# One planner, two orders: keeping column-tiled matmuls together in an agent-attention and SoLU-FFN kernel on Trainium2

## The chip, the cores and the metric

The kernel runs on one core of one Trainium2 chip. That core has a matrix engine (TensorE; the profile lists its matmuls as PE and its weight loads as PEld), three engines for elementwise work (VectorE as DVE, ScalarE as ACT, GpSimd as POOL) and a queue engine that issues all DMAs (SyncE as SP). Each engine executes its own instructions in the order in which they stand in the program. TensorE writes its results to PSUM, from where DVE and ACT read them. The metric is the device time of one execution in microseconds (us); less is better.

## The reference

Four batches, each with 12608 tokens of width 128. Stage one is agent attention with 49 agents per batch, stage two a feed-forward layer of width 1024 with a softmax-weighted activation (SoLU) and a layer norm:

```python
scale = 1.0 / np.sqrt(q.shape[-1])
def sm(a, b):
    s = scale * (a @ b.transpose(0, 2, 1))
    s = s - s.max(-1, keepdims=True)
    e = np.exp(s)
    return e / (e.sum(-1, keepdims=True) + 1e-09)
agent_v = sm(agents, k) @ v            # (4, 49, 128): over 12608 keys
x = (sm(q, agents) @ agent_v).reshape(B * S, D)

h = x @ w_in                           # (50432, 1024)
e = np.exp(h - h.max(-1, keepdims=True))
solu = h * e / (e.sum(-1, keepdims=True) + 1e-09)
mu = solu.mean(-1); var = ((solu - mu) ** 2).mean(-1)
out = ((solu - mu) / np.sqrt(var + 1e-06) * g_ln) @ w_out
```

Inputs and output are float32; `w_in` and `w_out` come as float64 words that the kernel converts itself (`pair_f64`).

## The kernel before, in words

The tokens are cut into 396 tiles of 128, 99 per batch. Three groups of steps are interleaved.

**The agents' stage (`phase_a`)** goes over the keys and values of one batch in 13 chunks of 1024 (the last has 320 keys). For chunk `c`: `p1_mm` (L418) multiplies agents and keys, `p1_max` and `p1_nm` (L423 to L430) keep a running maximum, `p1_exp` (L444) takes the exponentials, `p2_t` (L451) transposes them on TensorE, `p2_et` (L457) copies the transposed block out of PSUM on ACT or DVE, `p2_mm` (L467) multiplies with the values and `p2_ev` (L474, L476) adds it to the sum. At the end the sum is multiplied with `w_in` (`f3`, L531), so that the matrix of stage two already holds the agents' values. For batch 0 this stage runs alone, ahead of everything else: the head. For batches 1 to 3 it is woven into the tiles of the batch before.

**The queries' stage (`phase_b`)** goes over units of 8 tiles. `b0` (L647) multiplies 8 tiles of queries with the agents, `b1` to `b4` are the softmax, `b5` (L682) transposes, and DMAs lay the result out as `pT` (L706).

**The feed-forward stage** is done tile by tile: `c_h` (L747) makes h in PSUM, `c_max` (L751) the row maximum on DVE, `c_exp` (L761) on ACT, `c_u` (L766) on DVE, `c_sq` (L772) on ACT, `c_t` (L779) transposes u in eight blocks on TensorE, `c_ev` (L794, L798) copies on ACT, the parts are split into a high and a low half (L803 on DVE, L807 and L811 on POOL), and `c_w` (L827) does 24 matmuls with `w_out` for each pair of tiles.

On TensorE these steps use the array in two ways. `p1_mm`, `p2_mm` and `b0` write 64 of the 128 output rows with each matmul, two matmuls side by side: the array is tiled in columns, and the profile shows them as 128*64. All others (`c_h`, `c_w` and the transposes) use the whole array, shown as 128*128. The program numbers the kinds: 0 for `c_h` and `c_w`, 1 for transposes and a few small matmuls, 2 for the three column-tiled steps.

The order is made by a planner that runs when the program is built (class `Plan`). Each step is an `Op` with an engine, a planned duration (`cost`), a due time (`due`), the steps it waits for, and the PSUM bank that it takes or frees. `run` walks all engines: for each it looks at the steps that could start, keeps those that could start within `EPS[e]` of the earliest, and takes the one that is due first; of the engines, the one whose step starts first. After a TensorE step it adds `SWITCH[kind before][kind now]` to the planned duration. The order found so is the program's order on each engine; the chip then waits on semaphores alone. Planned durations and due times therefore set the order and nothing else; no instruction gets longer or shorter by them. Due times are built from constants such as `BD0` to `BD5` (queries' stage), `DH`, `DMX`, `DEX` and the like (tile steps), `ASTART` and `AEND` (agents' stage).

In the head the planner also puts filler matmuls (L918, into a PSUM tile that nobody reads) where it plans TensorE to stand idle, as many as fill 0.7 of the planned gap. The head further holds the conversion of both weights from float64 words (`pair_f64`, L263: per weight 18 instructions on DVE, 2 on ACT, 4 on POOL). `load_out` issues the load of `w_out` after the loads of chunk `VA`; the conversion of `w_out` must end before `c_exp` of the first two tiles, since it uses their buffers.

PSUM has four banks (`px`) for everything but h: `c_w` holds one over two pairs of tiles, and the column-tiled steps, the transposes and the small matmuls share the rest.

## Time and profile before

| | us |
|---|---|
| median of 3 runs | 1548.81 (1548.41 to 1549.6) |
| the profiled execution, its own time | 1548.65 |
| its span in the profile | 1546.9 |

The profiled execution's time is 1.75 us more than its span. Its stages, from the timeline: the head lasts to 62 us, where the first `c_h` stands; batches 0 to 2, each with the next batch's agents' stage woven in, last to about 1200 us; batch 3 has no agents' stage beside it and lasts to the end. The granted TensorE clock is 1.00 in every stage. A row of the timeline gives the start of the first of several equal instructions, the time from there to the end of the last, and their count. Matmuls are pipelined, each lasts longer than the distance to the next: what a matmul costs the engine is the distance between starts, not the duration in the row.

### The profile page before, as it was taken

The numbers are of one execution on the slowest core, as the hardware profiler recorded it, in microseconds if no ns is written. First come the engines' busy times: TensorE is split into PE (matmuls) and PEld (weight loads), VectorE is DVE, ScalarE is ACT, GpSimd is POOL, SyncE is SP. The second block draws the span as 40 slices with busy tenths as digits, with TensorE's granted clock in tenths as the row PEclk, the third lists the DMA queues.
The fourth block names the chain that finished last, engine by engine and source line by source line (L and its number), as shares of the span: only waits on it lengthen the run. The fifth ranks groups of instructions, "written<-read, shape, count | busy, mean of one in ns | idle before, by whom it ended". The sixth has DMA issues, their size and how long they took to land.

```text
span 1546.9 us, 35512 instructions
## 1 busy us (share of the span) xinstructions
PE 1526.4 (99%) x12628; PEld 1356.1 (88%) x12628; DVE 1372.4 (89%) x2214; ACT 1421.6 (92%) x2738; POOL 1252.9 (81%) x1613
## 2 busy tenths in 40 slices
PE   8899999999999999999999999999999999999998
PEld 4588898998889889898898889898889999999998
DVE  6988998888898889898898889889899999999997
ACT  3599999999899999999999999999999999999997
POOL 1478878787888887888878887887788899898987
PEclk9999999999999999999999999999999999999999
DMA  9533333324233333332333334433222232222221
GB/s 370 186 104 100 107 98 115 117 69 127 81 97 118 103 110 117 112 102 83 106 98 101 111 97 117 116 100 105 78 76 75 68 90 76 71 82 70 68 62 46
DMA packets 114721, 159.65 MB, mean 103 GB/s; under 512 B 16240, under 2 KB 71152, under 8 KB 114544
## 3 DMA queue, kind: packets, MB, share of 16 engines
q1 hardware_dynamic: 114544, 157.39, 34.0%
q8 instruction: 100, 1.64, 0.4%
q14 instruction: 77, 0.63, 0.1%
HBM read 105.36 MB, written 26.02 MB: 85 GB/s over the span
## 4 chain that ended last, share of the span: by engine, by line
PE 95%; DVE 3%; ACT 1%; DMA 1%; issue 0%; SPq 0%; DVEq 0%; ACTq 0%
PE px L827 36%; PE ph L747 24%; PE px L779 23%; PE px L647 3%; PE px L467 3%; PE px L418 3%; PE px L451 1%; PE px L682 1%; PE px L531 0%; DMA pT<-pn 0%; DVE mxp L423 0%; DVE nm L751 0%; DMA kh<-in_kT_dram 0%; DVE ca_in L263 0%; DVE uL L803 0%
## 5 line engine op out<-in xcount | busy, mean ns | idle before, releaser
L811 POOL TENSOR_TENSOR uL<-uT,uH 128x1024 fp32r<-128x1024 f32 (+1 forms) x344 | 661.5, 1923 | 27.6
L751 DVE TENSOR_REDUCE nm<-ph 128x1 f32<-128x1024 f32 x396 | 481.3, 1217 | 50.5 <-PE ph L747 47.7
L766 DVE SCALAR_TENSOR_TENSOR u<-ph,e 128x1024 f32<-128x1024 f32 x396 | 479.0, 1217 | 34.6 <-ACT e L761 24.4
L772 ACT ACTIVATE sq<-u,su 128x1024 bf16<-128x1024 f32 x396 | 460.5, 1163 | 24.8 <-DVE u L766 20.4
L761 ACT ACTIVATE e<-ph,nm 128x1024 f32<-128x1024 f32 x396 | 445.9, 1128 | 31.9 <-DVE nm L751 30.7
L827 PE MATMUL px<-uL,wH 128*128 128x256 f32 x1584 | 466.9, 295 | 0.2 <-POOL uL L811 0.2
L827 PE MATMUL px<-uH,wH 128*128 128x256 f32 x1584 | 450.6, 284 | 1.8 <-DVE uL L803 1.8
L827 PE MATMUL px<-uH,wL 128*128 128x256 f32 x1584 | 448.1, 283 | 0.0
L779 PE MATMUL px<-ident,u 128*128 128x128 f32 x3168 | 425.5, 274 | 2.7 <-DVE uL L803 1.4
L779 PEld LDWEIGHTS px<-ident,u 128*128 128x128 f32 x3168 | 356.7, 141 | 55.2 <-issue 20.7
L807 POOL TENSOR_SCALAR uH<-uT 128x1024 fp32r<-128x1024 f32 (+1 forms) x344 | 298.3, 867 | 98.4 <-ACT uT L798 98.0
L747 PE MATMUL ph<-mh,pT 128*128 128x512 f32 x792 | 329.7, 416 | 1.6 <-DMA pT<-pn 1.3
L827 PEld LDWEIGHTS px<-uH,wH 128*128 128x128 f32 x1584 | 299.0, 189 | 16.9 <-issue 3.5
L747 PE MATMUL ph<-ml,pT 128*128 128x512 f32 x792 | 312.3, 394 | 0.0
L798 ACT COPY uT<-px 128x512 f32<-128x512 f32 x541 | 299.2, 589 | 11.9 <-PE px L779 3.0
L827 PEld LDWEIGHTS px<-uH,wL 128*128 128x128 f32 x1584 | 299.1, 189 | 8.6 <-issue 0.7
L827 PEld LDWEIGHTS px<-uL,wH 128*128 128x128 f32 x1584 | 298.9, 189 | 8.5 <-issue 4.6
L803 DVE TENSOR_TENSOR uL<-px,uH 128x512 fp32r<-128x512 f32 x251 | 168.8, 685 | 47.5 <-ACT uH L794 45.8
L747 PEld LDWEIGHTS ph<-mh,pT 128*128 128x128 f32 x792 | 149.3, 188 | 20.3 <-issue 3.4
L747 PEld LDWEIGHTS ph<-ml,pT 128*128 128x128 f32 x792 | 149.9, 189 | 17.7 <-issue 0.5
L794 ACT CAST uH<-px 128x512 fp32r<-128x512 f32 x251 | 143.7, 592 | 1.2 <-PE px L779 0.9
L846 POOL TENSOR_TENSOR y<-x,nhalf 128x4 f32<-128x4 f32 x99 | 100.1, 1011 | 7.7
(118 smaller groups left out, 1337.6 us busy)
## 6 DMA issues: line engine op xcount, KB each, us to landing
pT<-pn SPq DMA_DIRECT2D x392, 64.0 KB
rB<-dr SPq DMA_DIRECT2D x98, 256.0 KB
qt<-in_qT_dram SPq DMA_DIRECT2D x48, 512.0 KB
out_dram<-ob SPq DMA_DIRECT2D x95, 256.0 KB
kt<-in_kT_dram SPq DMA_DIRECT2D x36, 512.0 KB
vt<-in_v_dram SPq DMA_DIRECT2D x36, 512.0 KB
dr<-yr SPq DMA_DIRECT2D x392, 0.5 KB
kh<-in_kT_dram SPq DMA_DIRECT2D x12, 512.0 KB
```

Of the source, the lines that this page charges most:

```text
L747: nc.tensor.matmul(ph[:, sl], lhs, bmats[b]["mh" if m == 0 else "ml"][:, sl], start=(m == 0), stop=(m == 1))
L751: nc.vector.tensor_reduce(out=nms[x], in_=phs[x], op=ALU.max, axis=AX.X, negate=True)
L761: nc.scalar.activation(out=es[x], in_=phs[x], func=AF.Exp, bias=nms.pop(x), accum_out=st[G]["S"][:, j : j + 1])
L766: nc.vector.scalar_tensor_tensor(out=u, in0=phs[x], scalar=INV, in1=es[x], op0=ALU.mult, op1=ALU.mult, accum_out=su)
L772: nc.scalar.activation(out=sq, in_=u, func=AF.Square, bias=su, scale=-float(DF), accum_out=st[G]["Q"][:, j : j + 1])
L779: nc.tensor.transpose(pt[:, kf * P : (kf + 1) * P], us[x][0][:, k0 * P : (k0 + 1) * P], ident)
L794: nc.scalar.copy(out=uH, in_=pt)
L798: nc.scalar.copy(out=rr[x][:, hf * 4 : hf * 4 + 4, :], in_=pt)
L803: nc.vector.tensor_tensor(out=uL, in0=pt, in1=uH.bitcast(F32), op=ALU.subtract)
L807: nc.gpsimd.tensor_scalar(out=uH, in0=rr[x][:, k0:k1, :], scalar1=1.0, scalar2=0.0, op0=ALU.mult, op1=ALU.add)
L811: nc.gpsimd.tensor_tensor(out=uL, in0=rr[x][:, k0:k1, :], in1=uH.bitcast(F32), op=ALU.subtract)
L827: nc.tensor.matmul(po, wt[:, kf, :], ut[:, kf, :], start=(q == 0), stop=(q == WM - 1))
```

## The change

The planner gets a new rule and new numbers. The rule: when TensorE's last planned step was column-tiled (kind 2), the planner first looks for column-tiled steps that could start within `HOLD` = 0.17 of the earliest step of any kind, and takes one of those if there is one. `SWITCH` now charges for going into column tiling (0.12) and for leaving it (0.18 and 0.14), and nothing for staying. The planned costs of the three column-tiled steps are set anew, and three of the conversion's DVE steps are planned at 0.9 for 0.6. The agents' stage of batches 1 to 3 is no longer spread evenly from `ASTART` to `AEND`: chunk `c` is due `UB * ASP` = 6.8 tiles after the one before, and its `p2_mm` is due later in that step (`MZ` = 2.36 for 1.5, where the next chunk's `p1_mm` stands at 2.55). `w_out` is loaded after chunk 9 for 7, `w_in` ahead of all keys (`WA`), the conversion of `w_in` is due after the agents' stage of batch 0 (`CPR`), not before it. Most of the other due times are new numbers.

```diff
--- before.py
+++ after.py
@@ -30,7 +30,9 @@
            "AA": 0.0, "AG": 0.17, "GP": 0.25, "GD": 0.1, "GG": 0.1, "GA": 0.2}
     EPS = {"P": 0.01, "A": 0, "D": 0.07, "G": 2.6, "S": 0.0}
 
-    SWITCH = ((0.0, 0.0, 0.0), (0.0, 0.0, 0.0), (0.087, 0.033, 0.033))
+    SWITCH = ((0.0, 0.0, 0.12), (0.0, 0.0, 0.12), (0.18, 0.14, 0.0))
+
+    HOLD = 0.17
 
     def __init__(self, banks):
         self.banks = [[0.0, b] for b in banks]
@@ -78,7 +80,10 @@
                     low = s if low is None else min(low, s)
                 if low is None:
                     continue
-                s, o = min((z for z in opts if z[0] <= low + self.EPS[e]), key=lambda z: z[1].due)
+                near = [z for z in opts if z[0] <= low + self.EPS[e]]
+                if e == "P" and self.kind == 2:
+                    near = [z for z in opts if z[0] <= low + self.HOLD and z[1].kind == 2] or near
+                s, o = min(near, key=lambda z: z[1].due)
                 if o.shy > 0.0:
                     s, o = min((z for z in opts if z[0] <= s + o.shy), key=lambda z: z[1].due)
                 if best is None or s < best[0]:
@@ -148,7 +153,7 @@
     CKT = N - NCK * CT * P
     AP2 = 64
     ETE = "AD"
-    CPR = -1.98
+    CPR = 1.32
     UTB = 4
     DIR = {(1, 0), (1, 1), (3, 1), (5, 1), (7, 1)}
     LGC = 8
@@ -156,56 +161,58 @@
     TD = 2
     WC = 4
 
-    BD0 = 13.69
-    BD1 = 8.27
-    BD2 = 9.96
-    BD3 = -18.57
-    BD4 = 0.41
-    BD5 = 5.85
-    DH = -3.05
-    DMX = -3.31
-    DEX = 7.76
-    DU_ = 6.48
-    DSQ = 21.68
+    BD0 = 14.77
+    BD1 = 12.82
+    BD2 = 19.94
+    BD3 = -16.84
+    BD4 = 0.17
+    BD5 = 4.61
+    DH = -3.24
+    DMX = 6.49
+    DEX = 0.49
+    DU_ = -2.17
+    DSQ = 18.46
     DT = -0.42
-    DEV = -6.42
-    DLD = 1.96
-    DSP = 2.68
-    DW = 3.31
-    DR = 2.33
-    DF_ = 5.14
-    OUTD = -5.86
+    DEV = -7.32
+    DLD = 2.24
+    DSP = -1.16
+    DW = 3.3
+    DR = 15.18
+    DF_ = 5.63
+    OUTD = -4.87
     OUTC = -74.58
-    VA = 7
+    VA = 9
     VA1 = 12
-    QA = 8
-    WA = 0.5
-    VLAG = 0.25
+    QA = 5.64
+    WA = -5.59
+    VLAG = 0.61
     PTB = 8
-    SHY = -2.99
-    DHR = -4.59
-    DHL = -5.42
-    DMXR = 10.02
-    DMXL = 15.46
-    DEXR = 5.1
-    DEXL = -1.93
-    DUR = -10.64
+    SHY = -0.0
+    DHR = -4.39
+    DHL = -5.43
+    DMXR = -0.03
+    DMXL = 10.25
+    DEXR = 23.76
+    DEXL = -1.81
+    DUR = -10.37
     DUL = -12.84
     DSQR = -10.36
     DSQL = -12.17
     DTR = -6.53
-    DTL = -23.81
-    DEVR = -0.65
+    DTL = -23.89
+    DEVR = -12.92
     DEVL = 9.51
     DLDR = -16.59
     DLDL = 26.96
     DSPR = -6.09
-    DSPL = 14.43
-    DWR = 0.63
+    DSPL = 14.3
+    DWR = 2.02
     DWL = -0.21
     RBL = 6.0
-    ASTART = -3.67
-    AEND = -2.04
+    ASP = 0.85
+    MZ = 2.36
+    ASTART = -3.92
+    AEND = -6.25
     engs = (mybir.EngineType.PE, mybir.EngineType.Activation, mybir.EngineType.DVE, mybir.EngineType.Pool)
     SCALE = 1.0 / math.sqrt(C)
     INV = 1.0 / DF
@@ -273,10 +280,10 @@
             + op("D", ts, "s", 0.34, in0="e", scalar1=23, scalar2=None, op0=SL)
             + op("D", ts, "a", 0.34, in0="hi", scalar1=12, scalar2=9, op0=SL, op1=SR)
             + op("G", gt, "r", 1.23, in0="r", in1="s", op=ALU.mult)
-            + op("D", tt, "a", 0.6, in0="s", in1="a", op=ALU.bitwise_or)
-            + op("D", stt, "a", 0.6, in0="lo", scalar=29, in1="a", op0=SR, op1=ALU.bitwise_or)
+            + op("D", tt, "a", 0.9, in0="s", in1="a", op=ALU.bitwise_or)
+            + op("D", stt, "a", 0.9, in0="lo", scalar=29, in1="a", op0=SR, op1=ALU.bitwise_or)
             + op("G", gt, "d", 1.23, in0="r", in1="a", op=ALU.add)
-            + op("D", stt, "di", 0.6, in0="hi", scalar=-(2 ** 31), in1="di", op0=ALU.bitwise_and, op1=ALU.bitwise_or)
+            + op("D", stt, "di", 0.9, in0="hi", scalar=-(2 ** 31), in1="di", op0=ALU.bitwise_and, op1=ALU.bitwise_or)
         )
         return ops[::2], ops[1::2]
 
@@ -550,7 +557,7 @@
         sz = lambda c: 0.524 if c < NCK else 0.164
         fr = lambda c: 1.0 if c < NCK else 0.5
         total = NC * 2.55 + 5.0
-        at = lambda z: due[0] + (due[1] - due[0]) * z / total
+        at = lambda z: due[0] + (due[1] - due[0]) * z / total if head else due[0] + UB * ASP * z / 2.55
         bg = op("G", begin, 0.0, at(0), gate)
         K, M1, E1, N1, V, M2, EE, TT, ET, AC = ({} for _ in range(10))
 
@@ -571,7 +578,7 @@
             if not head:
                 kop(c + 1)
             z = c * 2.55
-            M1[c] = op("P", st(p1_mm, c), (0.876 if c < NCK else 0.449) + (0.8 if head and c == 0 else 0.0), at(z),
+            M1[c] = op("P", st(p1_mm, c), (0.95 if c < NCK else 0.51) + (0.8 if head and c == 0 else 0.0), at(z),
                        [K[c], M1.get(c - 1), TT.get(c - 2)], take=True, kind=2)
             E1[c] = op("D", st(p1_max, c), 0.6, at(z + 0.3), [M1[c], bg])
             N1[c] = op("D", st(p1_nm, c), 0.07, at(z + 0.4), [E1[c], N1.get(c - 1)])
@@ -581,7 +588,7 @@
             TT[c] = op("P", st(p2_t, c), 0.435 * fr(c), at(z + 1), [EE[c], M2.get(c - 2)], take=True)
             ET[c] = op(ETE, st(p2_et, c), (0.478 * fr(c), 0.6 * fr(c)), at(z + 1.2), [TT[c]], free=TT[c])
             vop(c)
-            M2[c] = op("P", st(p2_mm, c), 1.043 if c < NCK else 0.485, at(z + 1.5),
+            M2[c] = op("P", st(p2_mm, c), 0.96 if c < NCK else 0.45, at(z + MZ) if not head else at(z + 1.5),
                        [ET[c], V[c], M2.get(c - 1), AC.get(c - 2)], take=True, kind=2)
             AC[c] = op("D", st(p2_ev, c), 0.26, at(z + 1.8), [M2[c], FC.get(c), AC.get(c - 1)], free=M2[c])
         if head:
@@ -711,7 +718,7 @@
         prev, first = None, None
         for j0, j1 in chunks:
             f = (lambda px, j0=j0, j1=j1: b0(j0, j1, px)) if prev is None else (lambda j0=j0, j1=j1: b0(j0, j1))
-            o = op("P", f, 0.155 * (j1 - j0), dues[0] + 0.1 * j0,
+            o = op("P", f, 0.128 * (j1 - j0), dues[0] + 0.1 * j0,
                    [BQ[k], prev, B0.get(k - 1)] + [B4.get((k - 2, q)) for q in range(2)] + list(gate), take=prev is None, kind=2, shy=shy)
             first = first or o
             prev = o
```

The numbers say little by themselves; the orders that the planner makes of them say more. Line numbers in the changed program are 7 higher.

TensorE in batch 1 around `p2_mm` of the agents' chunk 6 (values `vt_6`, keys `kt_`, queries `qt_`), before:

```order
L747 MATMUL ph_122<-ml_5821,pT_40_1_8367 128x512
L682 MATMUL px_124<-ident,pack_110 128x128 x2
L647 MATMUL px_125<-ag_sb,qt_56_7738 64x49 x16
L827 MATMUL px_127<-uH_8315,wH 128x256
L827 MATMUL px_127<-uL_8316,wH 128x256
L827 MATMUL px_127<-uH_8315,wL 128x256
L827 MATMUL px_127<-uH_8315,wH 128x256
L467 MATMUL px_126<-vt_6_7854,eT_6_8532 64x128 x8
L827 MATMUL px_127<-uL_8316,wH 128x256
L827 MATMUL px_127<-uH_8315,wL 128x256
```

The same chunk's `p2_mm` in the changed program:

```order
L834 MATMUL px_127<-uL_8314,wH 128x256
L834 MATMUL px_127<-uH_8313,wL 128x256
L474 MATMUL px_126<-vt_6_7899,eT_6_8466 64x128 x8
L654 MATMUL px_125<-ag_sb,qt_64_7585 64x49 x16
L425 MATMUL px_126<-kt_8_7906,ag_sb 64x512 x2
L754 MATMUL ph_123<-mh_5685,pT_40_1_8439 128x512
L754 MATMUL ph_123<-ml_5686,pT_40_1_8439 128x512
```

Before, `b0` and `p2_mm` stand apart with four `c_w` matmuls between them, and the next `p1_mm` follows three tiles later; now `p2_mm`, `b0` and `p1_mm` follow each other. Counted over the whole order, a stretch of column-tiled steps with whole-array steps on both sides occurs 142 times before and 67 times now: 18 and 15 in the head, 38 and 15 in batch 0, 36 and 17 in batch 1, 39 and 14 in batch 2, 11 and 6 in batch 3. The number of column-tiled matmuls is the same, and so is that of `c_h`, `c_w` and transposes. Filler matmuls: 92 before, 62 now. Twelve of the agents' stage's 48 full copies `eT` go from ACT to DVE (20 on DVE before, 32 now), and two of the four short ones from DVE to ACT.

SP at the start of the program (`kh` keys, `vh` values, `wd_in` the words of `w_in`), before:

```order
L396 DMA kh_0_135<-in_kT_dram 128x1024
L289 DMA wd_in_137<-in_w_in_dram 128x1024
L289 DMA wd_in_139<-in_w_in_dram 128x1024
L396 DMA kh_0_135<-in_kT_dram 128x1024
L407 DMA vh_0_142<-in_v_dram 128x1024
L396 DMA kh_2_144<-in_kT_dram 128x1024
L407 DMA vh_0_142<-in_v_dram 128x1024
```

And now:

```order
L296 DMA wd_in_135<-in_w_in_dram 128x1024
L296 DMA wd_in_137<-in_w_in_dram 128x1024
L403 DMA kh_0_139<-in_kT_dram 128x1024 x2
L403 DMA kh_2_142<-in_kT_dram 128x1024 x2
L414 DMA vh_0_145<-in_v_dram 128x1024
L403 DMA kh_4_147<-in_kT_dram 128x1024
L414 DMA vh_0_145<-in_v_dram 128x1024
```

The two halves of `w_in` (512 KB each) go ahead of the first keys. Further down, `w_out` (two loads of 512 KB) stood behind the keys and values of chunks 0 to 7; it now stands behind the keys of chunks 0 to 11 and the values of 0 to 9.

DVE at the start of the program, before (`mxp`, `nmp`: maximum of a chunk; `cm_in` to `cs_in`: conversion of `w_in`):

```order
L423 TENSOR_REDUCE mxp_130<-px_124 128x1
L428 TENSOR_SCALAR nmp_131<-mxp_130 128x1
L263 TENSOR_SCALAR cm_in<-wd_in_137 128x512
L263 TENSOR_SCALAR cm_in<-wd_in_139 128x512
L263 TENSOR_SCALAR ce_in<-wd_in_137 128x512
L359 TENSOR_TENSOR fold<-ident 128x64 x2
L457 COPY eT_0_218<-px_124 128x512
```

And now:

```order
L270 TENSOR_SCALAR cm_in<-wd_in_135 128x512
L270 TENSOR_SCALAR cm_in<-wd_in_137 128x512
L270 TENSOR_SCALAR ce_in<-wd_in_135 128x512
L270 TENSOR_SCALAR ce_in<-wd_in_137 128x512
L270 TENSOR_SCALAR ce_in<-ce_in 128x512 x3
L366 TENSOR_TENSOR fold<-ident 128x64 x2
L270 TENSOR_SCALAR ce_in<-ce_in 128x512
L270 TENSOR_SCALAR cs_in<-ce_in 128x512
L430 TENSOR_REDUCE mxp_130<-px_124 128x1
```

Nine conversion steps now stand before the first chunk's maximum. The conversion of `w_out` begins on DVE after the copy of chunk 10's block, where it began before the maximum of chunk 8.

## The prediction

> **What bounds the kernel now.** I read the page first: the engines' busy time, then the chain that ended last.
>
> ```profile
> PE 1526.4 (99%) x12628; PEld 1356.1 (88%) x12628; DVE 1372.4 (89%) x2214; ACT 1421.6 (92%) x2738; POOL 1252.9 (81%) x1613
> ...
> PE 95%; DVE 3%; ACT 1%; DMA 1%; issue 0%; SPq 0%; DVEq 0%; ACTq 0%
> ```
>
> TensorE is busy for 99% of the span, and 95% of the chain lies on it. But ACT stands at 92%, so the average does not say whether a faster TensorE would run into ACT. The busy time by stages does (stretch; then TensorE, weight loads, DVE, ACT, POOL, clock, DMA share, GB/s):
>
> ```profile
> 0.00:62.00 62.00, 52.07 (x469) 31.84 (x470) 45.52 (x106) 22.01 (x58) 19.00 (x29) 1.00 0.84 310
> 62.00:100.00 38.00, 34.63 (x296) 27.95 (x294) 34.36 (x56) 33.23 (x64) 25.55 (x31) 1.00 0.42 130
> 100.00:400.00 300.00, 298.54 (x2439) 265.10 (x2438) 266.78 (x428) 282.39 (x547) 247.25 (x318) 1.00 0.35 103
> 400.00:800.00 400.00, 398.71 (x3310) 356.76 (x3309) 355.17 (x574) 375.13 (x724) 327.70 (x421) 1.00 0.35 103
> 800.00:1200.00 400.00, 399.79 (x3316) 357.88 (x3316) 356.53 (x573) 376.07 (x723) 327.84 (x424) 1.00 0.34 98
> 1200.00:1500.00 300.00, 300.00 (x2485) 277.05 (x2485) 278.70 (x430) 296.24 (x560) 270.40 (x351) 1.00 0.26 74
> ```
>
> From 100 to 1200 us TensorE is idle for 1.5 + 1.3 + 0.2 = 3.0 us of 1100; ACT is busy for 94% there (375.13 of 400). What TensorE saves in these 1100 us comes off the end, as long as ACT does not fill up. From 1200 us on both are full (ACT 296.24 of 300, 98.7%). In the head TensorE is not the bound: it holds fillers, and DVE has 45.52 us of work.
>
> **What a stretch of column tiling costs.** "Busy" hides it, so I take distances between starts in the timeline. An agents' step `p1_mm` alone, then a `b0` alone, each between `c_w` matmuls (L827); then a `p2_mm` alone in front of transposes; last, an ordinary block of transposes:
>
> ```profile
> 160.58 0.28 PE L827 MATMUL px<-uH,wL 128*128 128x256 f32 x1
> 160.69 0.28 PE L827 MATMUL px<-uH,wH 128*128 128x256 f32 x1
> 160.90 1.08 PE L418 MATMUL px<-kt,ag_sb 128*64 128x512 f32 x4
> 161.91 0.39 PE L827 MATMUL px<-uL,wH 128*128 128x256 f32 x1
> 162.13 0.28 PE L827 MATMUL px<-uH,wL 128*128 128x256 f32 x1
> ...
> 168.53 0.28 PE L827 MATMUL px<-uH,wH 128*128 128x256 f32 x1
> 168.74 1.14 PE L647 MATMUL px<-ag_sb,qt 128*64 128x49 f32 x32
> 169.81 0.38 PE L827 MATMUL px<-uL,wH 128*128 128x256 f32 x1
> 170.03 0.28 PE L827 MATMUL px<-uH,wL 128*128 128x256 f32 x1
> ...
> 744.27 0.28 PE L827 MATMUL px<-uH,wH 128*128 128x256 f32 x1
> 744.48 1.09 PE L467 MATMUL px<-vt,eT 128*64 128x128 f32 x16
> 745.50 1.09 PE L779 MATMUL px<-ident,u 128*128 128x128 f32 x8
> 746.35 0.36 PE L827 MATMUL px<-uL,wH 128*128 128x256 f32 x1
> ...
> 819.83 1.03 PE L779 MATMUL px<-ident,u 128*128 128x128 f32 x8
> 820.62 0.37 PE L827 MATMUL px<-uH,wL 128*128 128x256 f32 x1
> ```
>
> And stretches that are already joined, one in the head (`p1_mm`, `p2_mm`, `b0`) and one in batch 1 (`b0`, `p1_mm`):
>
> ```profile
> 32.83 1.08 PE L418 MATMUL px<-kh,ag_sb 128*64 128x512 f32 x4
> 33.74 1.04 PE L467 MATMUL px<-vh,eT 128*64 128x128 f32 x16
> 34.61 1.09 PE L647 MATMUL px<-ag_sb,qt 128*64 128x49 f32 x32
> ...
> 487.77 1.14 PE L647 MATMUL px<-ag_sb,qt 128*64 128x49 f32 x32
> 488.74 1.04 PE L418 MATMUL px<-kt,ag_sb 128*64 128x512 f32 x4
> 489.72 0.39 PE L827 MATMUL px<-uL,wH 128*128 128x256 f32 x1
> 489.94 0.28 PE L827 MATMUL px<-uH,wL 128*128 128x256 f32 x1
> ```
>
> Two `c_w` matmuls start 0.11 us apart. *Going in*: from the last `c_w` to the first column-tiled matmul 0.21, in all three cases, so 0.10 more. *Going out*: `p1_mm` takes 1.01 alone and 0.91 with a column-tiled step behind it; `b0` 1.07 and 0.97; so 0.10. *Just after*: the first `c_w` holds the engine for 0.22, 0.11 more; eight transposes 0.85 for 0.79, 0.06 more. *The first pair*: `p2_mm` takes 1.02 alone and 0.87 with neighbours on both sides; 0.10 of these 0.15 is the going out, 0.05 is its start. A stretch fewer saves 0.10 + 0.10 + (0.06 to 0.11) + (0 to 0.05): 0.26 to 0.36 us. I take 0.30, since in the trace most stretches go over into transposes.
>
> **The change part by part.**
>
> *Joined steps.* The changed order has 23 stretches fewer in batch 0, 19 in batch 1, 25 in batch 2: 67 x 0.30 = 20 us off TensorE. Batch 3 has 5 fewer, 1.5 us. The matmuls themselves are the same in number and shape.
>
> *What this can set waiting.* A joined `p2_mm`, `b0`, `p1_mm` takes three of the four `px` banks, `c_w` holds the fourth, and the next transposes need one of them. `p2_mm`'s is free after one DVE step, while the other two steps still run for 0.97 + 1.0 us. Behind the joined stretch at 487.77 the `c_w` come at their 0.22, without a wait. TensorE's wait from 100 to 1200 us is 3.0 us now. Bounds: nothing more, or 0.2 us behind each of the 46 stretches that now hold several kinds, 9 us. I take 2, near the lower end, since the joined stretches of this trace show none.
>
> *Batch 3.* ACT has 3.8 us of room in 300, so the 1.5 us fit, but any delay of ACT then shows. I take 0.8; bounds 0 and 1.5.
>
> *ACT and DVE.* These groups are the copies `eT`:
>
> ```profile
> L457 ACT COPY eT<-px 128x512 f32<-128x512 f32 (+1 forms) x29 | 17.1, 588 | 6.0 <-PE px L451 6.0
> L457 DVE COPY eT<-px 128x512 f32<-128x512 f32 (+1 forms) x23 | 15.0, 650 | 3.7 <-PE px L451 3.7
> ```
>
> Ten fewer on ACT: 10 x 0.588 = 5.9 us off it, and 10 x 0.65 = 6.5 us onto DVE. DVE has 11% idle from 100 to 1200 us (266.78 of 300 and the two rows behind it), some 122 us; that covers it. Without that cover it would cost 6.5 us. With 20 us off the stages, ACT would come to some 95% there, below the 98.7% at which batch 3 runs without a stall.
>
> *The head.* Now the chain there runs over DVE, not over the loads; from the chain in order of time, from DVE's timeline, and the row of a stretch of the head:
>
> ```profile
> 1.22 4.30 DMA kh<-in_kT_dram
> ...
> 12.28 1.67 DVE ce_in L263 x5
> ...
> 16.69 1.50 DVE ca_in L263
> ...
> 40.32 1.34 DVE ce_out L263 x3
> ```
>
> ```profile
> 7.67 0.69 DVE L423 TENSOR_REDUCE mxp<-px 128x1 f32<-128x512 f32 x1 [6.68 <-PE px L418]
> ...
> 64.33 1.23 DVE L751 TENSOR_REDUCE nm<-ph 128x1 f32<-128x1024 f32 x1 [0.17 <-PE ph L747]
> ```
>
> ```profile
> 8.00:10.00 2.00, 1.68 (x12) 1.14 (x10) 1.79 (x7) 1.36 (x2) 0.00 (x0) 1.00 1.03 414
> ```
>
> DVE starts at 7.67 us, converts `w_in` between the first chunks, later `w_out`, and reaches the first tile's maximum at 64.33. Now `w_in` is there first: the first keys landed 4.3 us after their issue, 1.05 MB at 0.41 MB per us (414 GB/s) take 2.6 us. So DVE can begin at about 5 us with conversions, and the first maximum comes at about 10.3, 2.6 later; the second chunk no longer waits behind seven conversions. DVE gains some 2.7 us at the start and loses fewer afterwards; but the conversion of `w_out` now begins after chunk 10, and `c_exp` of the first two tiles waits for its end, with H, the maxima and all further tiles queued behind. `w_out`'s load, four keys' and two values' loads later (6 x 0.524 MB / 0.41 = 7.7 us), is not what decides: it would still land ahead of chunk 10's step. Bounds: 3 us longer (all of the later keys, nothing won), 8 us shorter (DVE's 6.7 us of idle ahead of its first step gone, and a little more). I take 4 shorter, between them, since the work on DVE is the same and only its gaps can go. Fillers go only where TensorE waits anyway: 30 fewer cost and bring nothing.
>
> *New planned costs and due times* move order alone; what they do is in the counts above.
>
> **The sum.** 1546.9 - 20 + 2 - 0.8 - 4 = 1524.1 us of span. The profiled execution's own time, 1548.65, is 1.75 over its span and 0.16 under the median shown: 1526.
>
> **The rivals.**
>
> *The head gains nothing* (12%): the keys come 2.6 us later and this lasts through the head, 3 us for -4. For it: the loads run without a gap at 414 GB/s. Against it: the chain goes over DVE. 1526 + 7 = 1533.
>
> *Half of the gain goes into waits* (11%): the readers of PSUM become the bound behind each joined stretch, half of 22.8 is left: 1537.
> The Trainium skill, "TensorEngine Tiling (Array Packing)", section Performance Considerations (PSUM Bottleneck), says that tiling makes TensorE faster but not the emptying of PSUM, which may then bind. By that rule the joined steps would give this rival's time; the row at 489.72 shows none of it so far.
>
> *Slower* (6%): at the joined stretches the next transposes wait for a bank. `p1_mm`'s is free only after a DVE maximum, a small DVE step and an ACT exponential, and each may queue behind a 1.2 us tile step. 46 stretches hold several kinds; without my 2 us the gain is 24.8, so it decides from 24.8 / 46 = 0.54 us each. At 0.7 each, 32 us: 1524 + 32 = 1556. Against it: tiles can go on with `c_h` and `c_w`, which need no new bank.
>
> *Nothing happens* (3%): column-tiled steps with other weights empty the array between them as well, and the head gives nothing: 1548. Against it: 0.91 and 0.87 us in the joined stretch.
>
> *More* (7%): the head gives 8, no new waits, and 0.33 for each of 67 stretches (2 more): 1526 - 4 - 2 - 2 = 1518.
>
> **How the numbers follow.** The forecast, 1526, has 61%; its own range is 1519 to 1532. The range 1516 to 1538 takes in "more", the head and the halved gain, and leaves the two cases of 9% out, with a little below. About 0.2%, 3.1 us, is what a measurement of this kernel can tell from no change. Faster: 61 + 12 + 11 + 7 = 91%; within 0.2%: 3%; slower: 6%.
>
> **What would show it.** Right: `p2_mm` takes about 0.87 us in joined stretches; the tiles of batches 0 to 2 take 1.7% less time each; TensorE's idle from 100 us to batch 3 stays below 6 us; ACT's share there comes to about 95%. Wrong: transposes (L786 then) with waits for DVE behind column-tiled steps; the first tile's maximum later than 64 us; ACT at 99% ahead of batch 3.

## The result, and the profile after

| | us |
|---|---|
| kernel before, beside it on the same chip | 1549.2 (1548.41 to 1550.54) |
| changed kernel, median of 4 runs | 1566.55 (1564.19 to 1567.63) |
| ratio | 1.0107, 95% interval 1.0093 to 1.0121 |
| span of the profiled execution, before and after | 1546.9 and 1564.9 |

The change makes the kernel 17 us slower. The forecast was 1526.

The page of the changed kernel: busy time by engine, and the shares of the chain of waits.

```profile
PE 1517.5 (97%) x12598; PEld 1353.7 (87%) x12598; DVE 1380.0 (88%) x2223; ACT 1418.4 (91%) x2729; POOL 1255.2 (80%) x1613
...
PE 22%; DMA 2%; DVE 1%; ACT 1%; issue 1%; SPq 0%; DVEq 0%; ACTq 0%
PE px L834 9%; PE px L786 6%; PE ph L754 6%; DMA rB<-dr 1%; PE px L654 1%; DVE ob L899 0%; DVE u L773 0%; ACT e L768 0%; PE px L689 0%; ACT uT L805 0%; ACT uH L801 0%; DVE nm L758 0%; ACT sq L779 0%; DMA dr<-yr 0%; DVE uL L810 0%
```

TensorE was busy for 1526.4 us before and is for 1517.5 now: less work, in a longer span (of the 8.9 us, 4.0 are the 30 filler matmuls fewer, 14.1 and 10.1 us). The shares of the chain add up to 27% only, so it covers only a part of the span; what it does show is new: a DMA, `rB<-dr`, and behind it `ob` on DVE. The busy time in the stretches that the prediction used (TensorE, weight loads, DVE, ACT, POOL, clock, DMA share, GB/s):

```profile
0.00:62.00 62.00, 52.02 (x481) 32.09 (x481) 47.81 (x108) 23.18 (x59) 16.72 (x28) 1.00 0.86 314
62.00:100.00 38.00, 30.90 (x228) 25.43 (x230) 31.23 (x55) 32.07 (x65) 26.83 (x31) 0.91 0.33 109
100.00:400.00 300.00, 292.07 (x2450) 261.56 (x2448) 263.38 (x419) 275.88 (x534) 242.37 (x310) 1.00 0.33 101
400.00:800.00 400.00, 393.07 (x3261) 353.71 (x3258) 354.93 (x575) 370.14 (x711) 323.04 (x415) 1.00 0.34 104
800.00:1200.00 400.00, 396.06 (x3313) 356.06 (x3311) 357.89 (x574) 373.56 (x719) 329.18 (x421) 1.00 0.31 97
1200.00:1500.00 300.00, 293.65 (x2434) 269.75 (x2432) 273.28 (x421) 288.91 (x546) 267.20 (x345) 1.00 0.24 73
```

From 100 to 1200 us TensorE is idle for 7.9 + 6.9 + 3.9 = 18.8 us, where it was 3.0; from 1200 to 1500 us for 6.4, where it was 0.0. ACT is busy for 1019.6 of these 1100 us, 93%, not more than before. So no engine has become the bound: TensorE waits. From 62 to 100 us it is idle for 7.1 us (3.4 before), and the granted clock is 0.91. The waits behind this, over the whole span (engine and line, what it waits for: us, times, longest):

```profile
DVE ob L899 <- DMA rB<-dr: 23.9, 18, 3.3
...
PEld px L786 <- DVE ob L899: 10.1, 11, 2.1
PE px L786 <- DVE u L773: 9.8, 3, 4.9
```

`ob` (L899) multiplies the product of four tiles with their layer-norm scale `rB`. The scale goes a long way: GpSimd works it out of the sums of the four tiles (L844 to L865), DVE transposes it (`yr`, L869), SyncE stores it to DRAM in four small DMAs (`dr`, L875) and loads it back broadcast to all partitions (`rB`, L876). All of these steps are due `DR` after the group's last tile, in the planner's count; the change moves it from 2.33 to 15.18, so they get a later place in the order. `ob` frees the `px` bank that `c_w` held. The group's row in the list of groups, of before and of after (busy and mean ns; idle ahead of it and what ended it):

```profile
L892 DVE TENSOR_TENSOR ob<-px,rB 128x512 f32<-128x512 f32 (+1 forms) x100 | 67.8, 679 | 4.5 <-ACT rB L883 2.1 <-PE ph L747 1.8 <-PE px L827 0.5
```

```profile
L899 DVE TENSOR_TENSOR ob<-px,rB 128x512 f32<-128x512 f32 (+1 forms) x100 | 67.8, 680 | 31.1 <-DMA rB<-dr 23.9 <-PE px L786 2.7 <-PE ph L754 1.6
```

Before, DVE never waited for the load; now for 23.9 us. One such wait in the changed kernel's timeline:

```profile
142.58 0.20 DVE L869 STREAM_TRANSPOSE yr<-ycol 128x32 f32<-128x32 f32 x1
142.81 1.27 SPq L875 DMA_DIRECT2D dr<-yr  x4
146.41 0.60 SPq L713 DMA_DIRECT2D pT<-pn  x1
147.18 0.48 SPq L876 DMA_DIRECT2D rB<-dr  x1
147.76 1.90 SPq L713 DMA_DIRECT2D pT<-pn  x3
...
152.62 0.69 DVE L899 TENSOR_TENSOR ob<-px,rB 128x512 f32<-128x512 f32 x1 [3.32 <-DMA rB<-dr]
153.23 1.21 DVE L773 SCALAR_TENSOR_TENSOR u<-ph,e 128x1024 f32<-128x1024 f32 x1
...
154.49 1.15 ACT L779 ACTIVATE sq<-u,su 128x1024 bf16<-128x1024 f32 x1 [2.83 <-DVE u L773]
...
154.50 0.50 PE L754 MATMUL ph<-mh,pT 128*128 128x512 f32 x1 [2.77 <-DVE u L773]
```

`yr` is ready at 142.78, the broadcast load is issued at 147.18, behind a `pT` DMA that itself stood until 146.41, and `ob` starts at 152.62, 9.8 us after `yr`. DVE executes in order, so `u` of the next tile stands behind `ob` (153.23); `u` frees the h banks, so `c_h` waits 2.77 us, and so does `sq` on ACT.

For the stages I add up distances between the starts of TensorE's instructions (a stage begins at the first `c_h` of a batch). "Waits" is what each distance has over the median distance, in the kernel before, between instructions of the same two kinds (TensorE's idle time, and whatever a lower clock adds); "rest" is the sum of these medians.

| us | head | batch 0 | batch 1 | batch 2 | batch 3 |
|---|---|---|---|---|---|
| before | 61.2 | 375.8 | 376.2 | 379.1 | 349.1 |
| of it waits | 10.3 | 11.5 | 3.3 | 3.5 | 2.9 |
| after | 54.9 | 385.6 | 384.4 | 377.8 | 355.5 |
| of it waits | 9.4 | 28.4 | 13.6 | 10.4 | 11.1 |

The rest falls from 1112.8 to 1095.3 us in batches 0 to 2: 17.5 us for 67 stretches fewer, 0.26 us each. The head is 6.3 us shorter. Waits grow by 17, 10, 7 and 8 us. The joining pays; the waits cost more. A further 1.2 us lie outside these stages.

### The profile page after: what moved, and what is told of

Same layout as the page of the kernel before. It is cut to its first block, busy times and chain, and to the rows that moved or that the text cites. A ratio compares the mean times of both kernels' runs of the same rounds, so it can differ in the third digit from the quotient of the medians.

```text
span 1564.9 us, 35459 instructions
## 1 busy us (share of the span) xinstructions
PE 1517.5 (97%) x12598; PEld 1353.7 (87%) x12598; DVE 1380.0 (88%) x2223; ACT 1418.4 (91%) x2729; POOL 1255.2 (80%) x1613
## 5 line engine op out<-in xcount | busy, mean ns | idle before, releaser
L773 DVE SCALAR_TENSOR_TENSOR u<-ph,e 128x1024 f32<-128x1024 f32 x396 | 480.0, 1218 | 41.2 <-ACT e L768 28.4
L768 ACT ACTIVATE e<-ph,nm 128x1024 f32<-128x1024 f32 x396 | 447.4, 1134 | 30.7 <-DVE nm L758 29.2
L786 PE MATMUL px<-ident,u 128*128 128x128 f32 x3168 | 431.9, 275 | 17.9 <-DVE u L773 9.8
L805 ACT COPY uT<-px 128x512 f32<-128x512 f32 x541 | 303.4, 592 | 18.2 <-PE px L786 8.8
```

The source lines that it names most:

```text
L768: nc.scalar.activation(out=es[x], in_=phs[x], func=AF.Exp, bias=nms.pop(x), accum_out=st[G]["S"][:, j : j + 1])
L773: nc.vector.scalar_tensor_tensor(out=u, in0=phs[x], scalar=INV, in1=es[x], op0=ALU.mult, op1=ALU.mult, accum_out=su)
L786: nc.tensor.transpose(pt[:, kf * P : (kf + 1) * P], us[x][0][:, k0 * P : (k0 + 1) * P], ident)
L805: nc.scalar.copy(out=rr[x][:, hf * 4 : hf * 4 + 4, :], in_=pt)
```

## The experiments: the scale

**The scale taken off the path.** All DMAs and steps stay, `ob` multiplies with ones, so the layer-norm scale is left out of the output:

```diff
-                                in1=st[G]["rB"][:, j0:j1], op=ALU.mult)
+                                in1=unit[:, j0:j1], op=ALU.mult)
...
```

> The changed kernel, with its order on every engine kept, but c_fin multiplies with a constant tile of ones instead of rB; the scale is still computed and loaded, only not used, so the output lacks the layer norm's scale. Late scale (the new DR lets rB land when DVE needs it, DVE stands at c_fin, and u, c_t and c_h stand behind it): the 31 us of DVE's idle ahead of c_fin go, TensorE gets back 20 to 30 us, 1537 to 1547 us. Joined steps (readers of PSUM stand behind each joined stretch): 1564 to 1567, as the changed kernel. Other due times (all steps planned too tight): a part of it only, 1555 to 1562.

1543.89 us (1542.61 to 1548.49), ratio 0.9967 (0.9955 to 0.9979): 22.7 us less than the changed kernel, and faster than before. DVE's idle time ahead of `ob` falls from 31.1 to 0.5 us; batch 3's waits fall from 11.1 to 1.7.

**`DR` alone, both ways.** The changed kernel with the old number, then the kernel before with the new one:

```diff
-    DR = 15.18
+    DR = 2.33
```

> The changed kernel with DR alone at its old 2.33; the order is planned anew, with 77 stretches of column tiling. Late scale: rB lands some 13 us ahead of its use again, no wait of DVE for it; 1530 to 1542 us. Joined steps: 1560 to 1567. Other due times: 1552 to 1560.

```diff
-    DR = 2.33
+    DR = 15.18
```

> The kernel before with DR alone at the new 15.18; 143 stretches. Late scale: DVE waits for rB as in the changed kernel, slower than before by 10 to 30 us, 1559 to 1579. Joined steps: 1547 to 1551, as before, since nothing is joined. Other due times: 1549 to 1556.

The second behaves as a late scale would, with a greater loss than expected: 1586.15 us, ratio 1.0239 (1.021 to 1.0267); DVE's idle ahead of `ob` is 38.9 us, 29.2 of it for the load, and batch 2 is 30 us longer. In this batch TensorE is idle for 17.1 us (0.2 before), 15.4 of them for a bank that `ob` frees; and behind such waits the granted clock is 0.50 for 20.5 us, which adds some 10 us more (an estimate: at half the clock, half of this time). But the first is worse still, and outside all three ranges expected: 1601.11 us, 1.0343 (1.0321 to 1.0366). Two of its waits:

```profile
POOL x L850 <- ACT sq L779: 56.1, 47, 5.3
POOL t L844 <- ACT e L768: 34.5, 23, 10.3
```

With an early due time the chain's first steps stand early on GpSimd and wait there for exponentials and squares, which the other new due times have put elsewhere; `x` waited for `sq` for 21.6 us in the changed kernel. TensorE then waits for `u`; that this comes from GpSimd's waits is argued from these rows, not shown by a run. So `DR` cannot be put back alone: among the other new due times the old number does worse than the new one.

**The planner told a longer way.** It counts 6 us from the first store to the scale's arrival (`RBL`); 10 instead:

```diff
-    RBL = 6.0
+    RBL = 10.0
```

> The changed kernel with the planner told that the scale takes 10 us to land in place of 6 (RBL); the order is planned anew. Late scale (the plan reckons with a landing that the chip does not keep): DVE's waits for rB go, 1538 to 1550. Any new order costs waits (the due times fit one order only): 1565 to 1600.

1570.39 us, ratio 1.0138 (1.0118 to 1.0158), slower than the changed kernel. DVE's idle ahead of `ob` does fall, to 7.9 us, since `ob` is now planned later. The bank of `c_w` is held for longer: from the last `c_w` to `ob` the median is about 5 us, 1.9 in the changed kernel and 0.8 before. But TensorE's waits for a bank that `ob` frees are 3.4 us, 8.8 in the changed kernel. What has grown is its wait of `c_h` for `pT`, 10.0 us for 4.8, with a longest of 4.0 us for 1.4; and the granted clock is 0.50 for 20.5 us of the tiles' time, 6.8 in the changed kernel. So the new order waits for something else; why `pT` comes later in it was not separated.

**One store instead of four.** This gives the scale a shorter way and leaves nothing out. The whole transposed tile goes out in one DMA; the load reads its first rows.

```diff
-            dr = dpool.tile([GT, P], F32, tag="dr", name=f"dr{G}")
+            dr = dpool.tile([SQB, P], F32, tag="dr", name=f"dr{G}")
-            for q in range(0, P, SQB):
-                nc.sync.dma_start(out=dr[:, q : q + SQB], in_=r["yr"][q : q + GT, :])
+            nc.sync.dma_start(out=dr.rearrange("j (q p) -> q j p", p=SQB), in_=r["yr"])
...
-                              in_=dr.rearrange("j p -> (j p)").unsqueeze(0).to_broadcast([P, P * GT]))
+                              in_=dr[:GT].rearrange("j p -> (j p)").unsqueeze(0).to_broadcast([P, P * GT]))
```

> The changed kernel, its order kept; the four stores by which a group's scale goes to memory (four issues, 1.28 us on SyncE) are one store of the whole transposed tile, so the broadcast load starts up to 1 us earlier. Theory (the scale comes too late in the changed kernel: VectorE stood 31 us ahead of the scaling in 26 gaps, and the product could be cheaper by about 22 us with a scale that is never late): each of some 25 gaps shrinks by up to 1 us, 1550 to 1558 us, and the waits of VectorE for the broadcast's load fall from 24 us to under 10. Rival (the lateness is set by when the chain's GpSimd and VectorE steps are placed, the stores' issue is not on its path): within 3 us of the changed kernel, 1563 to 1568.

1548.84 us (1545.26 to 1550.65), ratio 0.9988 (0.9978 to 0.9997): 17.7 us less than the changed kernel, 1.2 us below the theory's range and far from the rival. Its row:

```profile
L898 DVE TENSOR_TENSOR ob<-px,rB 128x512 f32<-128x512 f32 (+1 forms) x100 | 67.8, 679 | 8.9 <-DMA rB<-dr 5.7 <-ACT rB L889 1.0 <-PE px L786 1.0
```

And the same group of tiles in its timeline:

```profile
141.97 0.20 DVE L869 STREAM_TRANSPOSE yr<-ycol 128x32 f32<-128x32 f32 x1
142.20 0.57 SPq L874 DMA_DIRECT2D dr<-yr  x1
144.18 0.32 SPq L875 DMA_DIRECT2D rB<-dr  x1
145.81 2.66 SPq L713 DMA_DIRECT2D pT<-pn  x4
148.64 0.68 DVE L898 TENSOR_TENSOR ob<-px,rB 128x512 f32<-128x512 f32 x1
```

6.5 us from `yr` to `ob` for 9.8, and no wait. Why so much, where the issues take only 0.7 us less? "Its order kept" in the expectation holds for TensorE, DVE, ACT and GpSimd, whose orders are the same to the last instruction. It does not hold for SyncE, which the program does not tie to the plan (the list `engs` at the end of the diff's constants has the other four). In SyncE's order another DMA stands between stores and load for 80 of 98 groups before, 43 in the changed kernel and 22 here. No run takes the shorter issue and the new order on SyncE apart. The lags, from all groups (us):

| | before | after | one store |
|---|---|---|---|
| last `sq` of the group to `yr`, median | 5.7 | 14.4 | |
| first store to issue of the load, median / 90% | 3.3 / 4.5 | 2.8 / 4.8 | 2.0 / 3.6 |
| issue of the load to `ob`, median / smallest | 13.5 / 4.3 | 5.2 / 3.1 | 5.7 / 3.1 |

Before, the scale was there long before it was wanted, and the DMAs in between cost nothing. In the changed kernel the way is 2.8 (median) + 3.1 (the smallest lag to the use) = 5.9 us, just the 6 us that the planner counts, and up to some 8 where another DMA, such as a `pT` that waits for its data, stands ahead of the load on SyncE (4.8 + 3.1). The Trainium skill, "DMA: Bandwidth & Descriptors", section Anatomy of one DMA, gives a transfer that GpSimd issues a fixed cost of some 2 us, mostly for the receipt of the last write. The small store here is issued by SyncE, for which that section has no figure, and comes out close to it: its load is issued 1.95 us after it at the earliest.

What the one store leaves: TensorE is still idle for 10.9 us from 100 to 1200 us (18.8 in the changed kernel), and 6.8 of them are `c_h` waiting for `pT`, 4.8 there. So in this order the DMAs that lay out `pT` come next.

**Is it SyncE's time?** The one store in a kernel whose scale comes early (the joining in batches 0 to 2 on the kernel before, below):

> The joining in batches 0 to 2 on the kernel before, whose scale is early (planned due 2.33), with the one store of the scale. Theory (the one store is worth something only where the scale comes late): 1539 to 1542, as with four stores. Rival (it is SyncE's time or the queue, not the lateness, that the one store saves): 1530 to 1536.

1540.82 us, the same median as with four stores. The store is worth 17.7 us where the scale is late and nothing where it is not.

## The experiments: the joining

**Alone.** On the kernel before, only the rule, the switch costs, the agents' due times and the costs of the column-tiled steps:

```diff
+                near = [z for z in opts if z[0] <= low + self.EPS[e]]
+                if e == "P" and self.kind == 2:
+                    near = [z for z in opts if z[0] <= low + self.HOLD and z[1].kind == 2] or near
...
-    ASTART = -3.67
-    AEND = -2.04
+    ASP = 0.85
+    MZ = 2.36
+    ASTART = -3.92
+    AEND = -6.25
...
```

> The kernel before with the joining alone: the rule, HOLD, SWITCH, the column-tiled steps' planned costs, and the agents' stage timed in units; all other due times, the loads and the conversions as before; 78 stretches, 64 fewer. Late scale: the joining gives what it was priced at, 64 x 0.30 = 19 us less some waits, 1530 to 1537. Joined steps: slower than before, 1553 to 1565. Other due times: 1530 to 1540.

1564.03 us, ratio 1.0091 (1.0076 to 1.0106): by its time, what was expected if joined steps were the loss. By stages it is 62.3, 376.2, 376.8, 375.2 and 367.3: the loss is all in batch 3, where the joining has nearly nothing to join. The stretch from 1200 to 1500 us, and what waited for `u` from 1200 to 1540 us:

```profile
1200.00:1500.00 300.00, 293.41 (x2387) 268.16 (x2386) 270.52 (x415) 288.14 (x546) 260.84 (x336) 1.00 0.25 71
```

```profile
PEld px L786 <- DVE u L773: 5.3, 8, 1.3
PEld ph L754 <- DVE u L773: 5.1, 6, 1.8
...
PE px L786 <- DVE u L773: 3.5, 5, 1.1
PE ph L754 <- DVE u L773: 3.5, 4, 1.7
```

The rule, the cheaper `b0` and the switch costs together give the tiles of batch 3 another order (which of them does it was not separated), in which `u` comes just too late for `c_h` and the transposes. From 0.0 us of idle to 6.6, without a single instruction more.

**Alone, and only while there is something to join.** The same rule, costs and due times in batches 0 to 2; the head and batch 3 are planned with the old ones:

```diff
+        self.join = 0
...
-                    c += self.SWITCH[self.kind][o.kind]
+                    c += self.SWITCHES[self.join][self.kind][o.kind]
...
+                if e == "P" and self.kind == 2 and self.join:
...
-            o = op("P", f, 0.155 * (j1 - j0), dues[0] + 0.1 * j0,
+            o = op("P", f, (0.128 if 0 < k and b < B - 1 else 0.155) * (j1 - j0), dues[0] + 0.1 * j0,
```

> The kernel before with the joining alone, and that only while there is a next agents' stage to join (batches 0 to 2: rule, switch costs, q units' times, costs); head, batch 3 and every due time as before. Theory (the joining's own gain, about 16 us of spacing in batches 0 to 2, is real, and what eats it is where newly planned steps wait): the stages as the earlier runs had them, head 61.2, batches 376.2, 376.8, 375.2, and batch 3 as before at 349.1, sum 1538.5, with what lies around the span 1540; 1537 to 1546. Rival (due times fit one order only, so that batch 3 loses its 18 us whatever the rule does in it, since it starts from another state): 1552 to 1560.

1540.82 us (1540.08 to 1541.36), ratio 0.994 (0.9925 to 0.9955): the theory's sum gave 1540. That close a match is luck: the sum of the stages, 1538.5, leaves out 5.5 us of the span that lie around them (1541.4 for 1546.9 in the kernel before), so it should have given 1546, and batch 0 came out 5.7 us shorter than with the joining everywhere. The range holds, the rival's does not. This beats both kernels. Stages 60.5, 370.5, 376.6, 376.2 and 349.0. The rest of batches 0 to 2 is 15.7 us lower, for 62 stretches fewer (51 for 113); their waits are 7.9 us higher (11.7, 8.3, 6.2). So half of what the joining saves comes off the end.

## The experiments: the head

**The head's part alone**, on the kernel before:

```diff
-    CPR = -1.98
+    CPR = 1.32
-    VA = 7
+    VA = 9
-    QA = 8
-    WA = 0.5
-    VLAG = 0.25
+    QA = 5.64
+    WA = -5.59
+    VLAG = 0.61
-            + op("D", tt, "a", 0.6, in0="s", in1="a", op=ALU.bitwise_or)
+            + op("D", tt, "a", 0.9, in0="s", in1="a", op=ALU.bitwise_or)
...
```

> The kernel before with the head's part of the change alone: w_in ahead of the keys, its conversion due later, w_out two chunks later, the conversions planned longer. Late w_out: the head ends some 6 us earlier (61.2 to 55 us) and the first tiles lose most of it, 1545 to 1551. Head as forecast: 1543 to 1546. Any new order costs waits: 1560 or more.

1554.36 us, ratio 1.0029 (1.002 to 1.0039), in none of the three ranges. The head is 4.4 us shorter (56.8), batch 0 is 10.4 us longer, all else is as before. TensorE stands for 4.22 us ahead of the first tiles' transposes, for `u`. In the changed kernel, which has the same loads, there are two such waits, and more stands in the way; its timeline at the start of batch 0:

```profile
63.90 1.73 PE L786 MATMUL px<-ident,u 128*128 128x128 f32 x8 [3.32 <-DVE u L773]
...
68.24 0.39 PE L328 MATMUL px<-ws,ones 128*128 128x128 f32 x2
...
68.66 1.15 ACT L779 ACTIVATE sq<-u,su 128x1024 bf16<-128x1024 f32 x1 [2.42 <-PE px L328]
...
69.81 1.05 ACT L801 CAST uH<-px 128x512 fp32r<-128x512 f32 x2
70.41 1.29 DVE L810 TENSOR_TENSOR uL<-px,uH 128x512 fp32r<-128x512 f32 x2 [1.82 <-ACT uH L801]
...
73.13 1.23 DVE L773 SCALAR_TENSOR_TENSOR u<-ph,e 128x1024 f32<-128x1024 f32 x1
...
74.42 1.33 PE L786 MATMUL px<-ident,u 128*128 128x128 f32 x5 [4.87 <-DVE u L773]
```

`w_out` comes later, so its column mean (L328, which reads `ws`) runs 12.3 us after the first `c_h` (1.2 in the kernel before). `ws` has the buffer of `sq`. In the run with the head's part alone the first `sq` starts 0.3 us behind ACT's step before it; here it waits for the mean, ACT in order holds back `uH`, DVE in order holds back the next `u`, and TensorE stands for 4.87 us. It had stood for 3.32 us just before, and the clock followed; the stretches there:

```profile
62.00:70.00 8.00, 5.66 (x26) 4.65 (x26) 5.63 (x9) 4.57 (x10) 4.60 (x4) 0.79 0.35 121
70.00:78.00 8.00, 3.58 (x16) 3.29 (x17) 5.84 (x11) 6.97 (x13) 5.23 (x7) 0.79 0.00 0
78.00:100.00 22.00, 21.66 (x189) 17.50 (x189) 19.76 (x35) 20.53 (x43) 17.00 (x21) 1.00 0.45 145
```

The eight transposes at 63.90 take 1.73 us, 1.03 elsewhere. The Trainium skill, "TensorE: Matmul & The Clock Gate", section What's actually happening, says that the array falls to half its clock after an idle window of some 3.4 us and gets it back after as long a busy one. The trace agrees: each of the two waits, of 3.32 and 4.87 us, ends in a stretch of 8 us with a clock of 0.79, and there it is 0.50 for 3.41 us (64.19 to 67.61 and 74.43 to 77.85). But a window need not be idle throughout: in the run with the mean's buffer alone, below, the clock is 0.50 from 1036.46 to 1039.87 us, behind 3.41 us in which TensorE was busy for 1.38.

**The head's part without the later `w_out`** (`VA` = 7, all else as above):

> The kernel before with the head's part of the change (loads of q and w_in earlier, v's lag, conversions planned longer, planned time of the first products), but w_out loaded after chunk 7 as before. Theory (w_out's later load is what the first tiles wait for: its mean and its conversion stand in their way): the head still ends about 4 us earlier and batch 0 is within 3 us of before's, 1545 to 1549 us. Rival (the first tiles cannot start sooner than VectorE gives their u, whichever load comes first, so an earlier head end is given back): batch 0 again 8 to 12 us longer, 1552 to 1556.

1547.83 us, ratio 0.9985 (0.9976 to 0.9995), 6.5 us less than with it. Head 57.6, batch 0 379.7: the head gains 3.6 us and batch 0 gives 3.9 back (at most 3 was expected). The profiled execution shows no gain (span 1547.3 for 1546.9); the median is 2.0 us lower, and its interval only just leaves none out.

**The mean's buffer alone**, in the changed kernel:

```diff
-                pm["s"] = epool.tile([P, NF // 2, C], F32, tag="sq", bufs=1, name="ws")
+                pm["s"] = const.tile([P, NF // 2, C], F32, name="ws")
```

> The changed kernel, same order on every engine, but the partial sums of w_out (ws) have a buffer of their own, not that of sq; so ACT's first sq no longer waits for the mean of w_out on TensorE (2.4 us of idle there, and 4.9 us of TensorE's behind it at 69 us). Late w_out (its conversion, now after chunk 10, stands in the way of the first tiles): 3 to 6 us less than the changed kernel, 1560 to 1564. Late scale alone: 1565 to 1568, the same as the changed kernel.

1565.82 us, ratio 1.0109 (1.009 to 1.0128): nothing that can be told from the changed kernel. In the profile batch 0 is 3.5 us shorter: the wait of 4.87 us becomes 3.07, the one of 3.32 stays, and TensorE's busy time from 70 to 78 us rises from 3.58 to 5.78. So the buffer makes 1.8 us of that wait. Batch 2 is 3.8 us longer, though the order is the same on every engine, SyncE too: there TensorE waits for 1.81 us for a bank that `ob` frees, and behind this wait stands the 3.41 us at half the clock named above.

**The earlier `w_out` in the changed kernel**, without and with the one store:

```diff
-    VA = 9
+    VA = 7
```

> The changed kernel with w_out loaded after chunk 7 again, nothing else. Theory (the two chunks' delay of w_out costs the first tiles of batch 0, in the changed kernel as in the kernel before, where its undoing was worth 6.5 us): batch 0 shorter by about 6 us and the rest as in the changed kernel, 1558 to 1563. Rival (in the changed kernel the first tiles wait for VectorE's u whenever w_out comes, or the plan falls into another order that waits elsewhere): 1564 to 1570.

> The changed kernel with both mends, the one store of the scale and w_out after chunk 7. If the two losses are separate they add: 1566.6 less 17.7 less 6, 1540 to 1545. Rival (they overlap, or the earlier w_out only moves the first tiles' waits): 1546 to 1551.

Alone 1569.58 us, 1.012 (1.0103 to 1.0137), as the rival had it; with the one store 1545.37 us, 0.9964 (0.9951 to 0.9977), 3.5 us less than the one store alone, between the two ranges. So the earlier load, each time in an order planned anew, costs 3.0 us without the one store and gains 3.5 with it: what one mend is worth depends on the other. Alone, TensorE is idle for 4.3 us from 62 to 100 us instead of 7.1, but the groups wait for their scale (DVE's idle ahead of `ob` is 35.4 us for 31.1), the granted clock is 0.50 for 10.2 us of batch 0 (6.8 in the changed kernel, 3.4 with both mends), and batch 0 is 2.5 us longer than in the changed kernel.

**Joining and head together**, without the later `w_out`:

> The joining in batches 0 to 2 together with the head's part without the later w_out, on the kernel before. If both parts keep what they gain alone: 1534 to 1542 us. Rival (the two orders are planned into each other and the first tiles wait as in the changed kernel, or batch 3 loses again): 1550 to 1562.

1544.99 us, ratio 0.9968 (0.9955 to 0.9981): neither. The parts gained 9.0 and 2.0 us alone, and 4.9 together; batch 0 is 7.8 us longer than with the joining alone. In it TensorE is idle for 10.0 us, 5.2 with the joining alone, and the granted clock is 0.50 for 6.8 us, never there. Its longest wait, 2.71 us ahead of transposes of the first tiles, for `u`, stands in the run with the head's part alone as well.

**A control that settles nothing.** The changed kernel with `ws` in its own buffer, the scale replaced by ones, and every `rB` load reading the same 2 KB of DRAM, so that no load waits for a store (the output lacks the scale):

```diff
-                              in_=dr.rearrange("j p -> (j p)").unsqueeze(0).to_broadcast([P, P * GT]))
+                              in_=dz.rearrange("j p -> (j p)").unsqueeze(0).to_broadcast([P, P * GT]))
...
```

> The changed kernel, same order on TensorE and ACT, with three waits taken away: c_fin multiplies with ones and not with rB, rB is loaded from a constant in DRAM and so does not wait on SP for the scale's store, and ws has its own buffer. The output lacks the layer norm's scale. Late scale and late w_out together with SP's wait: 1544 less 3 to 6 for ws and 3 to 7 for pT that stood behind the scale's loads, 1531 to 1538. New due times (the order leaves too little room between a tile's own steps, whatever is detached): 1540 to 1545.

1577.49 us, ratio 1.0176 (1.0159 to 1.0194). Batches 1 to 3 are 380.4, 372.7 and 346.4, near those with the scale detached alone; batch 0 is 417.3. Its waits:

```profile
PEld ph L754 <- issue: 40.2, 16, 11.3
...
PE ph L754 <- DMA pT<-pn: 31.1, 6, 11.2
```

```profile
100.00:400.00 300.00, 269.38 (x2176) 243.17 (x2172) 235.08 (x370) 246.94 (x477) 214.18 (x276) 0.94 0.53 150
```

`pT` arrives late, and the DMA share from 100 to 400 us is 0.53 for 0.33. Whether that comes from loads issued earlier or from reading one place over and over was not settled, so this run says nothing of the late scale.

## Why the prediction was wrong

The account, from the medians (us):

| | |
|---|---|
| before, beside each of the five sets of runs | 1549.2 to 1550.6 |
| joining in batches 0 to 2, alone | -9.0 |
| head's part without the later `w_out`, alone | -2.0 |
| these two disturb each other | +6 |
| both together, measured (before: 1549.8) | 1545.0 |
| changed kernel with both mends, measured | 1545.4 |
| later `w_out`, in it (without the one store: -3.0) | +3.5 |
| late scale, in it (what the one store takes off) | +17.7 |
| changed kernel | 1566.6 |

That 1545.0 and 1545.4 agree is no proof that nothing else matters: the second has all the other new due times, and by stages the two differ by up to 5.8 us (batch 0, 378.3 and 372.5). What those due times cost or gain by themselves stays open.

*Joined steps, -20.* Right in kind, a little large: 0.26 us for each of 67 stretches, the lower bound given, 17.5 us. In the changed kernel's timeline of batch 1 a joined stretch looks as forecast:

```profile
492.09 1.09 PE L474 MATMUL px<-vt,eT 128*64 128x128 f32 x16
493.02 1.03 PE L425 MATMUL px<-kt,ag_sb 128*64 128x512 f32 x4
493.88 1.12 PE L654 MATMUL px<-ag_sb,qt 128*64 128x49 f32 x32
494.93 0.38 PE L834 MATMUL px<-uH,wH 128*128 128x256 f32 x1
495.15 0.29 PE L834 MATMUL px<-uL,wH 128*128 128x256 f32 x1
```

`p2_mm` takes 0.93 at the start of a stretch (1.02 alone), `p1_mm` 0.86 in the middle, and the `c_w` behind it come without a wait. (0.87 was given for a `p2_mm` with neighbours on both sides, read in the head; the one such `p2_mm` in the tiles takes 0.89.)

*What this can set waiting, +2, bounds 0 and 9.* This failed. By itself the joining cost 7.9 us of waits in batches 0 to 2 (1540.82), inside the bounds, and half of its gain, as in the rival of 1537, but not behind the joined stretches as that rival had it. In the changed kernel batches 0 to 2 wait 34 us longer. The place was wrong as well, banks taken by column-tiled steps: of the 18.8 us that TensorE is idle from 100 to 1200 us, 1.6 lie directly behind one (0.2 of 5.5 with the joining alone). 11.8 us are `c_h`, which I had named as what could go on meanwhile.

*"New planned costs and due times move order alone; what they do is in the counts above."* This is the step that failed most: it put the new due times at nothing. It is true that they move order alone, but an order is not priced by counting switches. One number, `DR`, put the scale's chain nine microseconds later (5.7 to 14.4), and I did not follow its DMAs through SyncE's queue: 17.7 us by the one store, 22.7 with the scale taken off the path. I followed TensorE, DVE and the head's loads, where the names of the change pointed.

*The head, -4.* The head ended 6.3 us earlier, and the first tile's maximum stands at 59.89 for 64.33. But an earlier end of the head is a gain only if the tiles behind it can run. That `w_out`'s load "is not what decides" was wrong: its place was worth 6.5 us in the kernel before and 3.5 in the changed one with the one store, though -3.0 without it. The mean behind it holds the buffer of the first `sq`, but that is 1.8 us of one wait; what else the later load does was not taken apart.

*Batch 3, -0.8.* It became +6.4: 1.8 us less of the rest, 8.2 more waits. "Any delay of ACT then shows" was the right warning with the wrong engine; it was the scale on DVE, since without it (one store) batch 3 is 347.1 us, 2.0 less than before.

*What would show it.* The tiles of batches 0 to 2 did not take 1.7% less but 1.5% more (1147.8 us for 1131.1), TensorE's idle was to stay below 6 us and came to 18.8, and ACT's share was to rise to 95% and fell to 93%: a bounding engine that waits leaves the others idle too. The joined steps became shorter and the first maximum came before 64 us, about as forecast, so these two were no test of the sum.

*The slower rival*, 1556, had transposes waiting for a bank. Transposes do wait for a bank, but for the one that `ob` frees when its scale has come (10.1 us of weight loads), not for the one behind `p1_mm`. Its time came nearer to the result than mine, by another mechanism.

## What to carry to other kernels

Read a change to a planner's numbers on every queue, also on the one that the plan does not tie down: for each chain that leaves an engine and comes back through DMAs, compare the time that it needs with the time that it had before (here 13.5 us from the load's issue to its use, where 3.1 can do) and ask what the new due time leaves. A due time taken alone out of a fitted set (`DR` back: 1601 us) tells more of the set than of itself; parts that stand alone, such as one DMA for four or the joining in three batches, tell what they are worth. Where the planner counts too short a time for such a chain, shorten the chain: telling the planner a longer time took DVE's wait away and made a new order that waits elsewhere, for `pT` above all (10.0 us for 4.8).
